# Product tiles of one step each, with a DMA transpose for every step, in an attention backward kernel

## The chip, the core and the metric

The kernel runs on one core of a Trainium2 chip. The metric is the device time of one execution in microseconds (us); lower is better. The time quoted for the kernel before is the median of three executions.

## What is computed

The reference runs a forward pass and its gradient. The forward pass takes a layer norm of `A_x` (2048 rows of 512), sends it through an attention block of 32 heads of 16 columns and through an MLP (512 to 1792 to 512, with gelu), gates one with the other and adds the input:

```python
def _A_ref(x, wqkv, wo):
    ...
    scores = jnp.einsum("bhqd,bhkd->bhqk", q, k) * (Dh ** -0.5)
    p = _softmax(scores, axis=-1)
    o = jnp.einsum("bhqk,bhkd->bhqd", p, v)
    ...
x = A_x
xn = _layernorm(x, axis=-1)
s = _A_ref(xn, A_wqkv, A_wo)
g = _silu(_B_ref(xn, B_w1, B_b1, B_w2, B_b2))
return x + s * g
...
_out, _vjp = jax.vjp(_f, A_x, A_wqkv, A_wo, B_w1, B_b1, B_w2, B_b2)
_grads = _vjp(grad_out)
```

The outputs are the forward result and seven gradients: of the input, the two attention weights, and the weights and biases of the MLP.

## The kernel before

The program has three stages. A first one (`Pre`) computes the norms, the projections, the MLP and the gradient that enters the attention. The middle one (`attention_core`) does the attention forward and backward in one sweep. The last one (`phase3`) forms the weight gradients and the gradient of the input. The schedule is written out by hand: each engine executes its instructions in the order in which the Python code emits them, and only semaphores hold an engine back.

The change lies in `attention_core`. Its work is cut into 64 blocks: 16 pairs of heads by 4 chunks of 512 queries. A block has 16 steps, one for each 128 keys (`kb` from 0 to 15), so there are 1024 steps, numbered `g`. A step handles 128 keys by 512 queries for both heads of a pair (`hj` 0 and 1):

- `emit_s`: TensorE forms the scores `s` (L906), and ScalarE takes their exponential into `et` (L912). One `et` tile holds four steps.
- `emit_d`: TensorE forms the gradient of the probabilities, `d` (L924).
- `emit_mult`: VectorE multiplies `d` with `et` into the product tile `gts` (L941), one instruction of 128x512 for each head. A `gts` tile holds two steps (an even and an odd `kb`), and the pool `gtp` has three such tiles.
- `emit_dmat`: after every odd `kb`, SyncE (SP) issues a DMA transpose (L956) of the whole `gts` tile, 128x2048 bf16, into a tile `gk` of the pool `gbp`. After every fourth step it also issues a DMA transpose `ekd` (L960) of one 128x512 part of `et`. So in four steps SP issues `gk`, `gk`, `ekd`.
- `emit_T` and `emit_cT`: TensorE transposes the other seven parts of `et` (L970), and ScalarE and VectorE copy them out as `ek` (L982).
- `emit_x`: TensorE accumulates `X` over the 16 steps (L1000, L1003, L1007); L1007 reads `gts`.
- `emit_xs`, `emit_XT`, `emit_fin`: once a block, `X` is copied out, transposed and finished by small GpSimd (POOL) operations at step 2 of the next block. These make the small weight tiles `W` (L1049 to L1055).
- `emit_z`: 20 steps behind, TensorE multiplies `gk` and `ek` by `W` into `Z` (L1080, L1088); `emit_acc` adds `Z` to an accumulator on VectorE (L1102).

A step's `gts` may be overwritten only when the DMA transpose that reads it has landed. L941 therefore waits for the landing of a transpose three tiles earlier, and the transpose on SP waits for the last of the products that it reads.

The operands of the next pair are loaded into a second set of tiles. The 13 loads are issued by POOL, one at a time, at steps 10, 14, 18, ... 58 counted from the first step of a pair. In front of each load POOL copies two elements of the current `gts` into `tick` (L1140), which holds the load back until VectorE has reached that step.

Other DMA transposes on SP are of use for comparison, because their sizes differ. `stg<-gp` (L679, in the last stage) is 128x2048 for the first three of its four column chunks, `CH = [(0, 4), (4, 4), (8, 4), (12, 2)]`, and 128x1024 for the fourth. `wT<-WKV_s` (L739) reads 128x1024 from device memory, and `wT<-in_A_wqkv_dram` (L738) 128x512.

Of the kernel before, what the change touches and what calls it, by code (L numbers as in the profile page):

```python
# [8 lines left out]
bf16 = mybir.dt.bfloat16  # L9
# [42 lines left out]
def op_load_list(k, t, p, ld):  # L52

    L = []
    for hj in range(2):
        h = 2 * p + hj
        L.append(lambda h=h, hj=hj: ld(out=t["KVT"][32 * hj + 1:32 * hj + 17, :], in_=k.KT_s[h * 16:h * 16 + 16, :]))
        L.append(lambda h=h, hj=hj: ld(out=t["QDT"][32 * hj + 1:32 * hj + 17, :], in_=k.QT_s[h * 16:h * 16 + 16, :]))
        L.append(lambda h=h, hj=hj: ld(out=t["QDT"][32 * hj:32 * hj + 1, :], in_=k.UT_s[h:h + 1, :]))
    for hj in range(2):  # L60
        h = 2 * p + hj
        L.append(lambda h=h, hj=hj: ld(out=t["KVT"][64 + 32 * hj:80 + 32 * hj, :], in_=k.VT_s[h * 16:h * 16 + 16, :]))
        L.append(lambda h=h, hj=hj: ld(out=t["QDT"][64 + 32 * hj:80 + 32 * hj, :], in_=k.DOT_s[h * 16:h * 16 + 16, :]))
    L.append(lambda: ld(out=t["NAT"][:].rearrange("q k j c -> q k (j c)"), in_=k.NAT_s[p]))
    L.append(lambda: ld(out=t["NATQq"][:].rearrange("q k j c -> q k (j c)"), in_=k.NATQq_s[p]))
    L.append(lambda: ld(out=t["NATQd"][:].rearrange("q k j c -> q k (j c)"), in_=k.NATQd_s[p]))
    return L
# [777 lines left out]
def attention_core(ctx, tc, k, Oall, dQall, dKVT_out, ident_f32, ident_bf, npairs=16, nqc=4):  # L845
    nc = tc.nc
    sb = lambda name, bufs: ctx.enter_context(tc.tile_pool(name=name, bufs=bufs, reuse_waits="tile"))
# [3 lines left out]
    ps_x = ctx.enter_context(tc.tile_pool(name="ps_x", bufs=1, space=PSUM, reuse_waits="tile"))  # L851
    ps_z = ctx.enter_context(tc.tile_pool(name="ps_z", bufs=1, space=PSUM, reuse_waits="tile"))
    etp = sb("etp", 3)
    gtp = sb("gtp", 3)
    gbp = sb("gbp", 12)
    ekd = sb("ekd", 6)
    ekc = sb("ekc", 7)
# [11 lines left out]
    tick = outp.tile([1, 2], bf16, name="tick")  # L869
# [12 lines left out]
    st_s, st_d, st_et, st_gt, st_T = {}, {}, {}, {}, {}  # L882
    blk = [dict(Gk={}, Ek={}) for _ in range(NB)]
    cur = {}

    def a_unit(g):
        return (g // 16, g % 16) if 0 <= g < NSTEP else None
# [6 lines left out]
    def op_of(j):  # L894
        return OP[blocks[j][0] % 2]

    def emit_s(g, hj):
        a = a_unit(g)
        if a is None:
            return  # L900
        j, kb = a
        op = op_of(j)
        qc = blocks[j][1]
        r = 32 * hj
        s = ps_st.tile([128, 512], f32, name="s", tag="st")
        nc.tensor.matmul(s[:], lhsT=op["KVT"][r:r + 32, kb * 128:(kb + 1) * 128], rhs=op["QDT"][r:r + 32, qc * 512:(qc + 1) * 512],  # L906
                         start=True, stop=True, tile_position=(r, 0))
        if hj == 0 and kb % 4 == 0:
            cur["et"] = etp.tile([128, 4, 2, 4, 128], bf16, name="et")
        et = cur["et"]  # L910
        st_et[g] = et
        nc.scalar.activation(out=et[:, :, hj, kb % 4, :], in_=s[:].rearrange("k (b q) -> k b q", b=4), func=ACT.Exp)  # L912

    def emit_d(g, hj):
        a = a_unit(g)
        if a is None:
            return
        j, kb = a
        op = op_of(j)
        qc = blocks[j][1]  # L920
        r = 64 + 32 * hj
        d = ps_d.tile([128, 512], f32, name="d", tag="d")
        st_d[g, hj] = d
        nc.tensor.matmul(d[:], lhsT=op["KVT"][r:r + 32, kb * 128:(kb + 1) * 128], rhs=op["QDT"][r:r + 32, qc * 512:(qc + 1) * 512],  # L924
                         start=True, stop=True, tile_position=(r, 0))
# [4 lines left out]
    def emit_mult(g):  # L930
        a = a_unit(g)
        if a is None:
            emit_cT(g - 1, 7 - VCOPY[(g - 1) % 16], 7, nc.vector.tensor_copy)
            return
        kb = a[1]
        if kb % 2 == 0:
            cur["gts"] = gtp.tile([128, 2, 2, 512], bf16, name="gts")
        gts = cur["gts"]
        st_gt[g] = gts
        for hj in range(2):  # L940
            nc.vector.tensor_tensor(out=gts[:, kb % 2, hj, :].rearrange("k (b q) -> k b q", b=4),  # L941
                                    in0=st_d.pop((g, hj))[:].rearrange("k (b q) -> k b q", b=4),
                                    in1=st_et[g][:, :, hj, kb % 4, :], op=ALU.mult)
            if hj == 0:
                emit_cT(g - 1, 7 - VCOPY[(g - 1) % 16], 7, nc.vector.tensor_copy)

    def emit_dmat(g):
        a = a_unit(g)
        if a is None:
            return  # L950
        j, kb = a
        kc = kb // 4
        if kb % 2 == 1:
            gk = gbp.tile([128, 2, 2, 4, 128], bf16, name="gk")
            blk[j]["Gk"][kb // 2] = gk
            nc.sync.dma_start_transpose(out=gk[:].rearrange("q r h b k -> q (r h b) k"), in_=st_gt[g][:].rearrange("k a h q -> k (a h q)"))  # L956
        if kb % 4 == 3:
            ek = ekd.tile([128, 4, 128], bf16, name="ekd")
            blk[j]["Ek"][(kc, 3)] = ek
            nc.sync.dma_start_transpose(out=ek[:], in_=st_et[g][:, 3, 1].rearrange("k a q -> k (a q)"))  # L960
# [15 lines left out]
    def emit_cT(g, lo, hi, copy):  # L976

        a = a_unit(g)
        if a is None or lo == hi:
            return  # L980
        j, kb = a
        copy(out=blk[j]["Ek"][kb // 4][:, kb % 4, lo:hi].rearrange("q i k -> q (i k)").bitcast(f32),  # L982
             in_=st_T[g][:, lo:hi].rearrange("q i k -> q (i k)").bitcast(f32))

    def emit_x(g, part):
        a = a_unit(g)
        if a is None:
            return
        j, kb = a
        if part == "e" and kb == 0:  # L990
            blk[j]["X"] = ps_x.tile([128, 512], f32, name="X", tag="X")
        X = blk[j]["X"]
        NATt = op_of(j)["NAT"]
        et = st_et[g]
        for c in range(4):
            half, hj = c // 2, c % 2
            r = 32 * c
            ev = et[:, half::2, hj, kb % 4, :]
            if part == "e":
                nc.tensor.matmul(X[r:r + 32, 0:256], lhsT=NATt[:, kb, hj, 1:33], rhs=ev,  # L1000
                                 start=(kb == 0), stop=False, skip_group_check=True, tile_position=(0, r))
            elif part == "l":
                nc.tensor.matmul(X[r:r + 32, 256:512], lhsT=Lc[:], rhs=ev,  # L1003
                                 start=False, stop=False, skip_group_check=True, tile_position=(0, r))
            else:
                gv = st_gt[g][:, kb % 2, hj, :].rearrange("k (b q) -> k b q", b=4)[:, half::2, :]
                nc.tensor.matmul(X[r:r + 17, 256:512], lhsT=NATt[:, kb, hj, 0:17], rhs=gv,  # L1007
                                 start=False, stop=(kb == 15), skip_group_check=True, tile_position=(0, r))

# [9 lines left out]
    def emit_XT(g):  # L1019
        j = g // 16 - 1  # L1020
        if g % 16 != FIN_AT or not 0 <= j < NB:
            return
        xs = blk[j].pop("xs")
        XT = ps_d.tile([128, 4, 128], f32, name="XT", tag="d")
        for qb in range(4):
            nc.tensor.transpose(XT[:, qb, :], xs[:, qb * 128:(qb + 1) * 128], ident_f32[:])
        blk[j]["XT"] = XT
# [84 lines left out]
    late = []  # L1112
    for hj in range(2):
        emit_s(0, hj)
    for g in range(NSTEP + 16 + 8):
        cur["g"] = g
        a = a_unit(g)
        if a is not None:
            j, kb = a
            p, qc = blocks[j]  # L1120
            if kb == 0 and qc == 0 and p + 1 < npairs:
                for i, f in enumerate(op_load_list(k, OP[(p + 1) % 2], p + 1, nc.gpsimd.dma_start)):
                    late.append((g + 10 + 4 * i, f))
        emit_s(g + 1, 0)
        emit_d(g, 0)
        emit_d(g, 1)
        emit_s(g + 1, 1)
        emit_T(g - 1)
        emit_XT(g)
        emit_z(g + ZOFF)  # L1130
        emit_x(g - 1, "e")
        emit_x(g - 1, "l")
        emit_x(g - 1, "g")
        emit_mult(g)
        emit_xs(g - 1)
        emit_fin(g)
        for it in [x for x in late if x[0] <= g]:
            late.remove(it)

            nc.gpsimd.tensor_copy(out=tick[:], in_=st_gt[g][0:1, kb % 2, 1, 510:512])  # L1140
            it[1]()
        emit_acc(g + ZOFF)
        emit_cT(g - 1, 0, 7 - VCOPY[(g - 1) % 16], nc.scalar.copy)
        st_T.pop(g - 1, None)
        emit_dmat(g)
        st_gt.pop(g - 2, None)
        st_et.pop(g - 12, None)
# [112 lines left out]
```

## Time and profile before

| | |
|---|---|
| median of three runs | 2374.84 us (2371.86 to 2382.14) |
| the profiled execution: time, span | 2376.85 us, 2375.1 us |
| first stage, `attention_core`, last stage (by the first and last rows of its tiles) | about 0 to 247, 247 to 1960, 1960 to 2375 us |
| TensorE (matmul) busy, whole span | 2186.0 us |
| VectorE busy, ScalarE busy | 1951.4 us, 1784.9 us |
| GpSimd busy | 619.5 us |
| granted TensorE clock, mean | 0.974 |
| data moved by DMA | 459.38 MB, mean 193 GB/s |

The profile shows one execution. A row of a group names the line, the engine, the operation and the tiles (`gts<-d,et` is written from `d` and `et`), then the number of instructions, their busy time and the mean of one, and the idle time in front of them with what ended it. SPq rows are the instructions of SP's queue: the duration of a DMA transpose there is the time that SP spends in issuing it, after its waits; the transfer itself ends later, and its landing is listed by tile. DMA queue q1 carries what SP issues, q0 what POOL issues, and the queues called "instruction" fetch program code. A "cycle" below is four steps.

### The profile page before, as it was taken

The page shows a single profiled execution, that of the slowest core. Times are in us where ns is not written, and L with a number is a line of the kernel's source. Part 1 is how long each engine was busy: PE and PEld are TensorE (multiplying, and loading weights), DVE is VectorE, ACT ScalarE, POOL GpSimd, SP SyncE. Part 2 cuts the span into 40 slices and gives each one's busy share as a digit, 9 for nine tenths or more (in the row PEclk, how much of TensorE's full clock was granted, in tenths as well). Part 3 has the DMA queues.
Part 4 walks back from the last instruction along what each step waited for, and adds up shares of the span by engine and source line. Part 5 has one row for each costly group of instructions (what it writes and reads, how often), then busy time and mean ns, then how long its engine had stood idle before and what let it go on. Part 6 is the DMA issues. An engine that isn't in the chain of part 4 may idle for free.

```text
span 2375.1 us, 79122 instructions
## 1 busy us (share of the span) xinstructions
PE 2186.0 (92%) x32738; PEld 1231.7 (52%) x32738; DVE 1951.4 (82%) x3760; ACT 1784.9 (75%) x3481; POOL 619.5 (26%) x1386
## 2 busy tenths in 40 slices
PE   6799899999999999999999999999999996698798
PEld 3444455555555555555555555555555553243353
DVE  5567799999999999999999999988999996687123
ACT  4554788988889888888988889888889976553112
POOL 4547322222222222221222223122222114200023
PEclk9999899999999999999999999999999998899899
DMA  6766899999999999999999999999999998694951
GB/s 216 228 223 213 177 193 185 199 194 188 192 195 192 187 193 191 196 188 191 192 188 193 194 197 191 189 185 187 195 198 198 191 184 274 159 264 134 261 171 52
DMA packets 1419418, 459.38 MB, mean 193 GB/s; under 512 B 1337134, under 2 KB 1401774, under 8 KB 1419056
## 3 DMA queue, kind: packets, MB, share of 16 engines
q1 hardware_dynamic: 1405008, 424.68, 93.9%
q0 software_dynamic: 12464, 28.06, 4.6%
q8 instruction: 256, 4.19, 0.7%
q10 hardware_dynamic: 1584, 1.57, 0.2%
q14 instruction: 106, 0.87, 0.1%
HBM read 60.69 MB, written 64.75 MB: 53 GB/s over the span
## 4 chain that ended last, share of the span: by engine, by line
PE 52%; DMA 18%; DVE 13%; ACT 8%; issue 4%; POOL 2%; SPq 2%; DVEq 0%; POOLq 0%; ACTq 0%
DMA gk<-gts 14%; PE tT L970 14%; PE s L906 8%; DVE gts L941 6%; PE Z L1080 5%; PE Z L1088 4%; ACT ek L982 3%; ACT et L912 3%; PE X L1000 3%; PE X L1003 3%; PE X L1007 3%; PE ps_dw L782 2%; PE ps_h L336 2%; PE ps_m L351 2%; PE ps_dw L606 1%
## 5 line engine op out<-in xcount | busy, mean ns | idle before, releaser
L941 DVE TENSOR_TENSOR gts<-d,et 128x512 bf16<-128x512 f32 x2048 | 1358.3, 683 | 129.6 <-DMA gk<-gts 48.4
L912 ACT ACTIVATE et<-s 128x512 bf16<-128x512 f32 x2048 | 1113.0, 595 | 140.1 <-PE s L906 89.7
L970 PE MATMUL tT<-ident_bf,et 128*128 128x128 bf16 x7168 | 574.2, 220 | 34.5 <-ACT ek L982 21.6
L970 PEld LDWEIGHTS <-et 128*128 128x128 bf16 x7168 | 440.9, 98 | 281.1 <-issue 272.6
L982 ACT COPY ek<-tT 128x320 f32<-128x320 f32 (+2 forms) x1024 | 479.8, 469 | 57.9 <-DVE ek L982 52.1
L906 PE MATMUL s<-QDT,KVT 32*128 32x512 bf16 x2048 | 458.2, 385 | 2.4 <-ACT et L912 1.7
L924 PE MATMUL d<-QDT,KVT 32*128 32x512 bf16 x2048 | 430.2, 387 | 24.1 <-DVE gts L941 22.9
L1003 PE MATMUL X<-et,Lc 128*32 128x256 bf16 x4096 | 292.0, 274 | 1.9 <-POOL Lc L866 1.9
L1000 PE MATMUL X<-et,NAT 128*32 128x256 bf16 x4096 | 292.0, 275 | 0.2 <-DVE xs L1016 0.2
L1007 PE MATMUL X<-gts,NAT 128*17 128x256 bf16 x4096 | 291.9, 274 | 0.0
L906 PEld LDWEIGHTS <-KVT 32*128 32x128 bf16 x2048 | 114.0, 91 | 269.9 <-issue 264.6
L1080 PE MATMUL Z<-gk,W 128*32 128x256 bf16 x4096 | 206.1, 279 | 5.4 <-DVE acc L1102 4.4
L1140 POOL COPY tick<-gts 1x2 bf16<-1x2 bf16 x195 | 34.0, 174 | 670.6 <-DVE gts L941 670.5
L1088 PE MATMUL Z<-ek,W 128*32 128x512 bf16 x1792 | 203.5, 391 | 0.1
L982 DVE COPY ek<-tT 128x128 f32<-128x128 f32 (+1 forms) x704 | 189.4, 269 | 0.2
L1049 POOL TENSOR_TENSOR W<-NATQq,rL 128x128 bf16<-128x128 bf16 x64 | 25.4, 397 | 555.8 <-DVE rL L1048 369.2
L1003 PEld LDWEIGHTS <-Lc 128*32 128x32 bf16 x4096 | 110.5, 97 | 51.9 <-POOL Lc L866 2.2
L1000 PEld LDWEIGHTS <-NAT 128*32 128x32 bf16 x4096 | 115.4, 97 | 12.7 <-issue 1.0
L1007 PEld LDWEIGHTS <-NAT 128*17 128x17 bf16 x4096 | 105.2, 92 | 2.4
L924 PEld LDWEIGHTS <-KVT 32*128 32x128 bf16 x2048 | 97.2, 91 | 4.3 <-issue 4.2
L1080 PEld LDWEIGHTS <-W 128*32 128x32 bf16 x4096 | 64.8, 94 | 58.7 <-issue 5.0
L592 ACT CAST ob_w<-ps_dw 128x512 bf16<-128x512 f32 (+1 forms) x22 | 12.4, 563 | 93.2 <-PE ps_dw L782 57.6
(193 smaller groups left out, 2461.5 us busy)
## 6 DMA issues: line engine op xcount, KB each, us to landing
gk<-gts SPq DMA_TRANSPOSE x512, 5.4
H1T_s<-h1r SPq DMA_DIRECT2D x28, 256.0 KB, 3.9
HGT_s<-hgT SPq DMA_DIRECT2D x8, 896.0 KB, 4.4
gp<-H1T_s SPq DMA_DIRECT2D x12, 512.0 KB, 5.0
DH_s<-stg SPq DMA_DIRECT2D x12, 512.0 KB, 3.5
hch<-DH_s SPq DMA_DIRECT2D x12, 512.0 KB, 7.8
out_dram<-ob_w POOLq DMA_DIRECT2D x42, 128.0 KB, 3.2
NAT_s<-NS SPq DMA_DIRECT2D x4, 1056.0 KB, 6.3
```

Of the source, the lines that this page charges most:

```text
L336: nc.tensor.matmul(ps[:], lhsT=w1_sb[:, ic, fc * 128:(fc + 1) * 128], rhs=yT[:, ic, g * 512:(g + 1) * 512], start=(ic == 0), stop=(ic == I ...
L906: nc.tensor.matmul(s[:], lhsT=op["KVT"][r:r + 32, kb * 128:(kb + 1) * 128], rhs=op["QDT"][r:r + 32, qc * 512:(qc + 1) * 512], start=True, ...
L912: nc.scalar.activation(out=et[:, :, hj, kb % 4, :], in_=s[:].rearrange("k (b q) -> k b q", b=4), func=ACT.Exp)
L924: nc.tensor.matmul(d[:], lhsT=op["KVT"][r:r + 32, kb * 128:(kb + 1) * 128], rhs=op["QDT"][r:r + 32, qc * 512:(qc + 1) * 512], start=True, ...
L941: nc.vector.tensor_tensor(out=gts[:, kb % 2, hj, :].rearrange("k (b q) -> k b q", b=4), in0=st_d.pop((g, hj))[:].rearrange("k (b q) -> k b ...
L970: nc.tensor.transpose(t[:, i, :], et[:, i // 2, i % 2, kk, :], ident_bf[:])
L982: copy(out=blk[j]["Ek"][kb // 4][:, kb % 4, lo:hi].rearrange("q i k -> q (i k)").bitcast(f32), in_=st_T[g][:, lo:hi].rearrange("q i k -> q ...
L1000: nc.tensor.matmul(X[r:r + 32, 0:256], lhsT=NATt[:, kb, hj, 1:33], rhs=ev, start=(kb == 0), stop=False, skip_group_check=True, tile_positi ...
L1003: nc.tensor.matmul(X[r:r + 32, 256:512], lhsT=Lc[:], rhs=ev, start=False, stop=False, skip_group_check=True, tile_position=(0, r))
L1007: nc.tensor.matmul(X[r:r + 17, 256:512], lhsT=NATt[:, kb, hj, 0:17], rhs=gv, start=False, stop=(kb == 15), skip_group_check=True, tile_pos ...
L1080: nc.tensor.matmul(Z[r:r + 32, h * 256:(h + 1) * 256], lhsT=WT[j % 2][1][:, qb, hj, :], rhs=blk[j]["Gk"][2 * kc + h][:, :, hj, qb, :], sta ...
L1088: nc.tensor.matmul(Z[r:r + 32, :], lhsT=WT[j % 2][0][:, qb, hj, :], rhs=mv, start=False, stop=(qb == 3), skip_group_check=True, tile_posit ...
```

## The change

The product tile now holds one step, and the pool has six of them instead of three tiles of two steps; the bytes are the same. After each step SP issues a DMA transpose of that step's 128x1024 into its half of `gk`. `gk` itself, its pool and its readers keep their shape, except that L1007 reads the new `gts`. The 13 operand loads of a pair move from steps 10, 14, 18, ... 58 to steps 6, 9, 12 and 15 of each block (6, 9, 12, 15, 22, 25, ... 54 from the first step of the pair).

```diff
-    gtp = sb("gtp", 3)
+    gtp = sb("gtp", 6)
...
         kb = a[1]
-        if kb % 2 == 0:
-            cur["gts"] = gtp.tile([128, 2, 2, 512], bf16, name="gts")
-        gts = cur["gts"]
+        gts = gtp.tile([128, 2, 512], bf16, name="gts")
         st_gt[g] = gts
         for hj in range(2):
-            nc.vector.tensor_tensor(out=gts[:, kb % 2, hj, :].rearrange("k (b q) -> k b q", b=4),
+            nc.vector.tensor_tensor(out=gts[:, hj, :].rearrange("k (b q) -> k b q", b=4),
...
-        if kb % 2 == 1:
-            gk = gbp.tile([128, 2, 2, 4, 128], bf16, name="gk")
-            blk[j]["Gk"][kb // 2] = gk
-            nc.sync.dma_start_transpose(out=gk[:].rearrange("q r h b k -> q (r h b) k"), in_=st_gt[g][:].rearrange("k a h q -> k (a h q)"))
+        if kb % 2 == 0:
+            cur["gk"] = gbp.tile([128, 2, 2, 4, 128], bf16, name="gk")
+            blk[j]["Gk"][kb // 2] = cur["gk"]
+        nc.sync.dma_start_transpose(out=cur["gk"][:, kb % 2].rearrange("q h b k -> q (h b) k"),
+                                    in_=st_gt[g][:].rearrange("k h q -> k (h q)"))
...
-                gv = st_gt[g][:, kb % 2, hj, :].rearrange("k (b q) -> k b q", b=4)[:, half::2, :]
+                gv = st_gt[g][:, hj, :].rearrange("k (b q) -> k b q", b=4)[:, half::2, :]
...
-                    late.append((g + 10 + 4 * i, f))
+                    late.append((g + 16 * (i // 4) + 6 + 3 * (i % 4), f))
...
-            nc.gpsimd.tensor_copy(out=tick[:], in_=st_gt[g][0:1, kb % 2, 1, 510:512])
+            nc.gpsimd.tensor_copy(out=tick[:], in_=st_gt[g][0:1, 1, 510:512])
```

## The prediction

> **What bounds the kernel now.** I read first the page's busy times and its chain of work, then the middle stage by itself, then SP's queue, since the change doubles the transposes that SP issues. The page says:
>
> ```profile
> PE 2186.0 (92%) x32738; PEld 1231.7 (52%) x32738; DVE 1951.4 (82%) x3760; ACT 1784.9 (75%) x3481; POOL 619.5 (26%) x1386
> ...
> q1 hardware_dynamic: 1405008, 424.68, 93.9%
> ...
> q8 instruction: 256, 4.19, 0.7%
> ...
> DMA gk<-gts 14%; PE tT L970 14%; PE s L906 8%; DVE gts L941 6%; PE Z L1080 5%; PE Z L1088 4%; ACT ek L982 3%; ACT et L912 3%; PE X L1000 3%; PE X L1003 3%; PE X L1007 3%; PE ps_dw L782 2%; PE ps_h L336 2%; PE ps_m L351 2%; PE ps_dw L606 1%
> ```
>
> The largest member of the chain is no engine but the transfer `gk<-gts`, and SP's DMA queue q1 is busy for 93.9% of the span. The busy times by stretch show the middle stage:
>
> ```profile
> 247.00:1960.00 1713.00, 1645.54 (x29935) 976.14 (x29938) 1578.51 (x3071) 1507.98 (x3072) 398.14 (x1129) 0.99 1.12 191
> ```
>
> The columns after the length are PE, PEld, DVE, ACT and POOL. DVE is busy 1578.5 of 1713 us, so 134 us at most could be won there before it binds. In the waits DVE loses to the transposes only
>
> ```profile
> DVE gts L941 <- DMA gk<-gts: 48.4, 56, 2.2
> ```
>
> SP is on no busy list, so I looked at its queue in order of time, start and duration first (x2 merges two issues and the gap between them):
>
> ```profile
> 999.94 4.79 SPq L956 DMA_TRANSPOSE gk<-gts  x2
> 1004.83 1.21 SPq L960 DMA_TRANSPOSE ekd<-et  x1
> 1006.13 5.77 SPq L956 DMA_TRANSPOSE gk<-gts  x2
> 1011.99 1.22 SPq L960 DMA_TRANSPOSE ekd<-et  x1
> 1013.31 5.03 SPq L956 DMA_TRANSPOSE gk<-gts  x2
> 1018.45 1.80 SPq L960 DMA_TRANSPOSE ekd<-et  x1
> 1020.34 4.64 SPq L956 DMA_TRANSPOSE gk<-gts  x2
> ```
>
> Three cycles last 1020.34 - 999.94 = 20.40 us, and SP is inside them for 4.79 + 1.21 + 5.77 + 1.22 + 5.03 + 1.80 = 19.82 us. SP is nearly full already. How long one issue takes by size is told by the rows of single tiles and lines (durations are minimum/median/maximum in ns):
>
> ```profile
> L956 SPq DMA_TRANSPOSE gk<-gts x512: 1590/2190/5047, 251.0 to 1952.1; - x171
> ```
> ```profile
> L960 SPq DMA_TRANSPOSE ekd<-et x256: 1189/1219/2455, 258.8 to 1954.2; - x128
> ```
> ```profile
> L739 SPq DMA_TRANSPOSE wT<-WKV_s x4: 1307/1307/1309, 2204.3 to 2212.3; - x4
> ```
> ```profile
> L679 SPq DMA_TRANSPOSE stg<-gp x16: 1340/1627/2962, 2106.2 to 2189.1; - x16
> ```
>
> The undisturbed issue is some 1.20 us for 128x512, 1.31 (L739) to 1.34 (the shortest of `stg`, one of its 128x1024 ones) for 128x1024, and 1.59 to 1.61 for 128x2048. That is a straight line with a fixed part: 1.20 + (1.60 - 1.20)/3 = 1.33 for 128x1024. Four times the data cost a third more; two issues of half the size cost 2.67 where one cost 1.60. The rest of the 2.19 us median of `gk` is SP held up by the transfers behind it. That shows in the DMA view of 1006 to 1016 us, 40 slices of 0.25 us:
>
> ```profile
> GB/s 276 287 185 0 0 114 290 291 290 289 289 288 231 53 240 216 88 0 0 0 0 6 9 9 137 293 290 286 293 280 289 217 0 0 209 291 292 287 291 293
> ...
> q8 instruction: 1, 0.02, 0.7%
> ```
>
> At full rate, some 290 GB/s, the 512 KB of one `gk` take 1.8 us. For almost 2 us (from 1010) nothing moves, in a stretch that holds one fetch of program code (q8); SP's second issue of that pair, at 1008.23, took 3.67 us, and `gts` L941 stood still in front of 1012.41. By the packet records the stage has 279 such stalls of half a microsecond or more, about one a cycle.
>
> **The change part by part.**
>
> *SP's issues.* A cycle takes away two `gk` issues and adds four halves. Gaps between issues are 0.09 to 0.10 us (1004.83 + 1.21 to 1006.13). The least that SP needs in a cycle is before 2 x 1.60 + 1.22 + 3 x 0.10 = 4.7 us, under the 6.65 us that a cycle takes (1704.4 us from the first issue at 251.0 to the end of the last at 1955.4, by 256 cycles), so stalls of up to 1.9 us have room. After it is 4 x 1.34 + 1.22 + 5 x 0.10 = 7.08 us. That alone exceeds the present cycle by 0.43 us; by 256 cycles, +109 us. Nothing hides it: SP has no other place in the program for these issues, and every one is needed to free a product tile. With 1.307 us and gaps of 0.09 the least is 6.87, +57 us: the lower end.
>
> *What of the stalls stays on SP.* Before, SP's excess over the undisturbed issue is 0.71 us for a mean `gk` (the 512 records' mean is 2.31) and 0.05 for a mean `ekd` (1.27 against 1.22), though `ekd` is issued right behind a `gk` whose data are still moving. SP is thus held when much is outstanding, and little when little is. A half has 256 KB, 0.9 us of transfer in an issue of 1.44 us with its gap, so the engines drain each before the next is pushed; a stall must first be longer than that slack. Ends: 5 x 0.05 = 0.25 us a cycle by the row of `ekd`, 2 x 0.71 = 1.42 by the row of `gk`, if each stall stays whole on SP. Below nothing is excluded, since the undisturbed issue is the least there is. I take 0.25, because with idle time between transfers a half resembles `ekd` more than two `gk` back to back: 256 x 0.25 = +64 us. The upper end is 364 us.
>
> *Product tiles.* DVE's instructions keep their number and shape (2048 by 683 ns). A tile comes free when its own half has landed, where it had to wait for the pair. This could give back the 48.4 us, but only while SP keeps up. When SP is last, DVE runs into the six tiles and waits for landings; behind L941 on DVE stand the copies `ek` (L982) and the accumulation (L1102), and through them PE and ACT wait. So I credit nothing. The six-step depth stays: six steps of 7.08/4 = 1.77 us are 10.6 us, and a landing now takes 5.4 us (median), so the loop does not bind by itself. In the built program each SP transpose also waits for the transpose eight issues before it; eight were 10.7 steps and are 6.4, still 11 us. Covered; only landings beyond 11 us would cost.
>
> *Loads.* Number and size are the same: 195 ticks of 174 ns and 195 issues of about 0.5 us on POOL, which is busy 398 of 1713 us in the stage. Every fourth load used to sit at step 2 of a block behind the finishing operations, and now none does; PE has waited for POOL's `W` for 2.0 us in all. The last load moves from step 58 to 54, so nothing is late. I cost it at nothing; if that cover failed, it would be 0.7 us in front of `W` 64 times, 45 us.
>
> The sum: 2376.85 + 109 + 64 = 2550 for the profiled execution; its time is 2 us above the median of the runs, so 2548.
>
> The Trainium skill, page "DMA: Bandwidth & Descriptors", section "Issuing engines are not separate DMA queues", calls the sequencer time of an issue "usually small relative to the DMA itself". By that rule SP would have room and the change would cost nothing. The trace differs: 1.6 us of issue stand against 1.8 us of transfer. The same page, section "Rules for kernel authors", says to coalesce many small transfers into one; it speaks against this change, without a price for SP.
>
> **The rivals.** (1) SP is not the limit, and the earlier release of tiles counts. This decides if a half issues in (6.65 - 1.22 - 0.50)/4 = 1.23 us or less. Then DVE's 48.4 us go and the time is 2328. For it speaks the 14% of `gk<-gts` in the chain; against it the three sizes, none of which allows 1.23 at 128x1024. 9%. (2) An issue shrinks with its bytes, because what is measured is mostly waiting: 2.19/2 = 1.1 us, a cycle needs 6.1 us, DVE still paces, and nothing changes: 2375. Against it: `ekd` at a quarter of the bytes takes 1.22. 3%. (3) Each stall holds SP as long as now: 109 + 364 = 473 us, 2848. For it: the fetches come with PE's instructions, whose number is unchanged. Against it: the row of `ekd`. 8%.
>
> **How the numbers follow.** The forecast, SP as the pace, has 80%. Its own range runs from 2376.85 + 57 = 2434, a little less for gains that I do not credit, to an excess of 0.835 us a cycle, the middle between the ends: 2376.85 + 109 + 214 = 2700. I say 2425 to 2700, which leaves the rivals out. About 0.5%, 12 us, is what a measurement of this kernel can tell from no change. Faster by more: 0.09. Within: 0.03. Slower: 0.88.
>
> **What the profile after would show.** Right: SP's queue without gaps over 0.1 us, 1024 `gk` issues with a minimum near 1.34 us and a median little above it, the middle stage longer by 110 to 330 us, DVE's wait for `gk<-gts` grown to a hundred us or more, DMA with idle slices between transfers. Wrong: gaps on SP in front of each half (rival 1 or 2), or a median issue of 1.7 us and more (rival 3). If the first or the last stage changes, I have missed something.

## The result, and the profile after

The changed kernel takes 2632.22 us (median of four runs, 2626.03 to 2632.38), the kernel before 2375.36 (median of the three runs above and a fourth): a ratio of 1.1071, 95% interval 1.1042 to 1.1101. The profiled execution took 2626.03 us with a span of 2624.3 us. The forecast was 2548 in a range of 2425 to 2700: the direction and the mechanism held, the size fell short by 84 us.

The page of the changed kernel, the same lines as before. TensorE's busy share falls, and so does that of the DMA queue, while the transfer `gk<-gts` takes a quarter of the chain in place of 14%:

```profile
PE 2286.1 (87%) x32689; PEld 1269.6 (48%) x32738; DVE 1958.3 (75%) x3760; ACT 1788.9 (68%) x3481; POOL 624.8 (24%) x1386
...
q1 hardware_dynamic: 1421392, 424.75, 85.1%
...
q8 instruction: 256, 4.19, 0.7%
...
DMA gk<-gts 25%; PE tT L969 10%; PE s L906 6%; DVE gts L939 5%; ACT ek L981 4%; PE Z L1087 3%; PE Z L1079 3%; ACT et L912 3%; PE X L999 2%; PE X L1002 2%; PE X L1006 2%; PE ps_dw L782 2%; DVE ek L981 2%; PE ps_h L336 1%; PE ps_m L351 1%
```

No engine and no DMA queue is fuller than before, so what paces the kernel is not on these lines. The busy times of the middle stage (from the first `gk` issue to the end of the last `ekd` issue; columns as in the prediction) say where the time is. Of the two lines, the first is the kernel before, the second the kernel after, each from its own answer:

```profile
251.00:1955.40 1704.40, 1639.65 (x29835) 972.85 (x29835) 1574.83 (x3066) 1504.40 (x3065) 390.22 (x1115) 0.99 1.12 192
```
```profile
251.00:2197.10 1946.10, 1740.08 (x29889) 1010.08 (x29889) 1583.75 (x3067) 1508.35 (x3065) 400.42 (x1128) 0.97 1.00 168
```

The stage is 241.7 us longer, while VectorE and ScalarE do the same work in the same busy time, within 0.6%. TensorE's busy time grows by 100 us with the same instructions, at a mean granted clock of 0.97 in place of 0.99; whether that is a cause or a consequence is asked below (F). The rest of the program starts the stage at the same 251.0 us and needs 427.2 us behind it in place of 419.7. A cycle of four steps went from 6.66 to 7.60 us. SP's queue in order of time (x4 merges four issues and the gaps between them):

```profile
1005.32 6.83 SPq L954 DMA_TRANSPOSE gk<-gts  x4
1012.24 1.23 SPq L959 DMA_TRANSPOSE ekd<-et  x1
1013.59 6.66 SPq L954 DMA_TRANSPOSE gk<-gts  x4
1020.36 1.20 SPq L959 DMA_TRANSPOSE ekd<-et  x1
1021.66 5.70 SPq L954 DMA_TRANSPOSE gk<-gts  x4
1027.45 1.22 SPq L959 DMA_TRANSPOSE ekd<-et  x1
```

From 1005.32 to 1028.77, where the next issue starts, SP pauses once, for 0.40 us at 1016.96; all other gaps are 0.09 to 0.12 us. Over the whole stage the median gap is 0.09 us, and only 22 gaps of 1279 exceed 0.15 us; before there were 213 of 767. The rows by tile:

```profile
L954 SPq DMA_TRANSPOSE gk<-gts x1024: 1231/1262/3092, 251.0 to 2194.6; - x171
```
```profile
L959 SPq DMA_TRANSPOSE ekd<-et x256: 1188/1219/2977, 258.4 to 2195.9; - x128
```

A half issues in 1.26 us at the median where a pair took 2.19, but there are twice as many. VectorE's wait for the landing has grown from 48.4 to 187.7 us, though each tile is now released by itself:

```profile
DVE gts L939 <- DMA gk<-gts: 187.7, 177, 3.4
```

And the DMA engines are idle more often. This is the view of 1006 to 1016 us, 40 slices:

```profile
GB/s 0 0 0 4 8 10 12 12 193 290 292 241 22 0 131 184 278 254 293 253 259 282 284 138 91 280 292 287 138 12 234 315 29 0 0 182 271 69 16 79
```

Counted from the packet records between 260 and 1950 us in slices of 0.1 us, fewer than four packets are under way on average in 15% of the slices, against 8% before, though the bytes are the same. Not all of it is waiting for SP: the first gap of the view, 1006 to 1008, is a stall like that in the view of before, in a stretch that holds one fetch. But no engine of the kernel is nearer to its limit than before, and SP has no room left.

### The profile page after: what moved, and what is told of

Same layout as the page of the kernel before. It is cut to its first block, busy times and chain, and to the rows that moved or that the text cites. A ratio compares the mean times of both kernels' runs of the same rounds, so it can differ in the third digit from the quotient of the medians.

```text
span 2624.3 us, 80432 instructions
## 1 busy us (share of the span) xinstructions
PE 2286.1 (87%) x32689; PEld 1269.6 (48%) x32738; DVE 1958.3 (75%) x3760; ACT 1788.9 (68%) x3481; POOL 624.8 (24%) x1386
## 3 DMA queue, kind: packets, MB, share of 16 engines
q1 hardware_dynamic: 1421392, 424.75, 85.1%
## 4 chain that ended last, share of the span: by engine, by line
PE 42%; DMA 28%; DVE 12%; ACT 8%; issue 5%; POOL 2%; SPq 1%; DVEq 0%; POOLq 0%; ACTq 0%
DMA gk<-gts 25%; PE tT L969 10%; PE s L906 6%; DVE gts L939 5%; ACT ek L981 4%; PE Z L1087 3%; PE Z L1079 3%; ACT et L912 3%; PE X L999 2%; PE X L1002 2%; PE X L1006 2%; PE ps_dw L782 2%; DVE ek L981 2%; PE ps_h L336 1%; PE ps_m L351 1%
## 5 line engine op out<-in xcount | busy, mean ns | idle before, releaser
L939 DVE TENSOR_TENSOR gts<-d,et 128x512 bf16<-128x512 f32 x2048 | 1357.7, 684 | 352.7 <-DMA gk<-gts 187.7
L969 PE MATMUL tT<-ident_bf,et 128*128 128x128 bf16 x7168 | 589.6, 224 | 62.7 <-ACT ek L981 52.6
L969 PEld LDWEIGHTS <-et 128*128 128x128 bf16 x7168 | 451.8, 99 | 310.7 <-issue 303.4
L924 PE MATMUL d<-QDT,KVT 32*128 32x512 bf16 x2048 | 493.9, 392 | 122.9 <-DVE gts L939 120.1
L906 PE MATMUL s<-QDT,KVT 32*128 32x512 bf16 x2048 | 517.8, 393 | 2.3 <-ACT et L912 1.6
L906 PEld LDWEIGHTS <-KVT 32*128 32x128 bf16 x2048 | 127.8, 91 | 414.5 <-issue 409.5
L1002 PE MATMUL X<-et,Lc 128*32 128x256 bf16 x4096 | 297.4, 279 | 1.8 <-POOL Lc L866 1.8
L999 PE MATMUL X<-et,NAT 128*32 128x256 bf16 x4096 | 297.6, 280 | 0.2 <-DVE xs L1015 0.2
L1087 PE MATMUL Z<-ek,W 128*32 128x512 bf16 x1792 | 209.7, 402 | 0.1
L1079 PEld LDWEIGHTS <-W 128*32 128x32 bf16 x4096 | 68.8, 94 | 72.6 <-issue 17.8
L924 PEld LDWEIGHTS <-KVT 32*128 32x128 bf16 x2048 | 98.0, 91 | 11.5 <-issue 11.4
L1087 PEld LDWEIGHTS <-W 128*32 128x32 bf16 x2048 | 53.2, 93 | 59.5 <-issue 15.7
```

What stands on the lines that cost most here:

```text
L939: nc.vector.tensor_tensor(out=gts[:, hj, :].rearrange("k (b q) -> k b q", b=4), in0=st_d.pop((g, hj))[:].rearrange("k (b q) -> k b q", b=4 ...
L969: nc.tensor.transpose(t[:, i, :], et[:, i // 2, i % 2, kk, :], ident_bf[:])
L1002: nc.tensor.matmul(X[r:r + 32, 256:512], lhsT=Lc[:], rhs=ev, start=False, stop=False, skip_group_check=True, tile_position=(0, r))
L1079: nc.tensor.matmul(Z[r:r + 32, h * 256:(h + 1) * 256], lhsT=WT[j % 2][1][:, qb, hj, :], rhs=blk[j]["Gk"][2 * kc + h][:, :, hj, qb, :], sta ...
L1087: nc.tensor.matmul(Z[r:r + 32, :], lhsT=WT[j % 2][0][:, qb, hj, :], rhs=mv, start=False, stop=(qb == 3), skip_group_check=True, tile_posit ...
```

## The experiments

The theory (A): SP issues the transposes one after the other, an issue has a price that hardly falls with its size, and the changed kernel asks for five a cycle in place of three, which is more than fits. The rivals: the new load steps (C), the single tiles and their waits (D), the DMA engines moving small transposes less well (B), TensorE (F).

**Which part of the change it is.** `loads_only` is the kernel before with

```diff
-                    late.append((g + 10 + 4 * i, f))
+                    late.append((g + 16 * (i // 4) + 6 + 3 * (i % 4), f))
```

> The kernel before with the new load steps alone. Theory A (SP's issues pace the middle stage, the loads cost nothing): 2363 to 2387 us, the same as before within 0.5%. Rival C (part of the 257 us comes from the loads, which now collide with other work): 2400 us or more.

Measured: 2369.83 us against 2384.67 of the kernel before on the same chip, ratio 0.9935 (0.9916 to 0.9954). The loads cost nothing; they are worth 15 us, a little more than the 0.5% expected at most. Where those come from the profile cannot say: it caught the slowest of the six executions, 2376.89 us, with a stage of 1702.2 us, 2 us less than before, and a wait of VectorE for `gk<-gts` of 46.3 us in place of 48.4.

`split_old_loads` is the changed kernel with that line put back.

> The changed kernel with the old load steps, that is the split alone. Theory A: SP paces either way, so the load steps do nothing: 2615 to 2655, within 1% of the changed kernel's ratio of 1.107. Rival C (the load steps are worth 15 us in either direction there too): 2600 or 2650 and beyond.

Measured: 2638.74 us, ratio 1.1086 (1.1046 to 1.1127); 1.1071 with the new load steps. The two intervals overlap, and the load steps cannot be told from nothing there. The split alone makes the whole loss.

`split_pair_tiles` keeps the three tiles of two steps and splits only the DMA:

```diff
-            nc.sync.dma_start_transpose(out=gk[:].rearrange("q r h b k -> q (r h b) k"), in_=st_gt[g][:].rearrange("k a h q -> k (a h q)"))
+            for r in range(2):
+                nc.sync.dma_start_transpose(out=gk[:, r].rearrange("q h b k -> q (h b) k"), in_=st_gt[g][:, r].rearrange("k h q -> k (h q)"))
```

> The kernel before with its three tiles of two steps and the old load steps, but each tile is transposed by two DMAs of 128x1024, both issued after the odd step. Theory A (what counts is the number of issues on SP, 5 a cycle): 2600 to 2700 us, as the changed kernel, since SP has to do the same. Rival D (the six single tiles are what costs: their waits and releases): back to 2375 to 2420 us.

Measured: 2632.54 us, ratio 1.1036 (1.1007 to 1.1065). The halves issue as in the changed kernel:

```profile
L957 SPq DMA_TRANSPOSE gk<-gts x1024: 1231/1263/3237, 251.7 to 2213.5; - x171
```

Tiles, waits and releases are those of the kernel before, and the loss is that of the changed kernel. D falls. It also shows that the release by single steps returned no time that can be seen: with it 1.1086 or 1.1071, without it 1.1036. VectorE's wait for the landings does differ, 237.4 us here against 180.1 in `split_old_loads`; with SP as the pace, that is no gain.

**Issues or data.** `no_ekd` takes one issue in five out of the changed kernel:

```diff
-        if kb % 4 == 3:
-            ek = ekd.tile([128, 4, 128], bf16, name="ekd")
-            blk[j]["Ek"][(kc, 3)] = ek
-            nc.sync.dma_start_transpose(out=ek[:], in_=st_et[g][:, 3, 1].rearrange("k a q -> k (a q)"))
...
-                        if qb == 3 and hj == 1:
-                            mv = blk[j]["Ek"][(kc, 3)][:]
-                        else:
-                            mv = blk[j]["Ek"][kc][:, :, 2 * qb + hj, :]
+                        mv = blk[j]["Ek"][kc][:, :, min(2 * qb + hj, 6), :]
```

> The changed kernel without the ekd transposes; the last part of et goes into Z from another part of ek (output not the reference's). 4 issues a cycle. Theory A: 7.60 us a cycle less 1.22 + 0.10 for the issue and some 0.2 of its stalls is 6.1 us, under the 6.65 of before, so SP no longer paces and the time falls to 2340 to 2420 us. Rival B (data): 11% of the data in the stage, 1946 x 0.11 = 214 us at the most: 2410 to 2500.

Measured: 2312.81 us, ratio 0.9694 (0.9676 to 0.9711), a little below the 2340 expected. The kernel still makes four issues a cycle, one more than the kernel before, and has lost only the 11% of the transposed data that `ekd` had; yet it is some 320 us faster than the changed kernel, where rival B allowed 214 at the most. The loss is more than undone. The cycle is 6.41 us, of which the four issues take 5.90 and their gaps 0.51: SP is still full, but no longer late. VectorE's wait all but ends:

```profile
DVE gts L939 <- DMA gk<-gts: 3.9, 9, 0.8
```

`plain_copy` leaves bytes, tiles, waits and the number of DMAs as in the changed kernel and replaces the kind:

```diff
-        nc.sync.dma_start_transpose(out=cur["gk"][:, kb % 2].rearrange("q h b k -> q (h b) k"),
-                                    in_=st_gt[g][:].rearrange("k h q -> k (h q)"))
+        nc.sync.dma_start(out=cur["gk"][:, kb % 2].rearrange("q h b k -> q (h b k)"),
+                          in_=st_gt[g][:].rearrange("k h q -> k (h q)"))
```

> The changed kernel with a plain DMA copy of the same 256 KB in place of each half transpose (output not the reference's); ekd stays a transpose. Bytes, number of issues, tiles and waits are the same; a plain issue took 0.32 to 0.57 us on SP elsewhere in the trace. Theory A: SP needs 4 x 0.45 + 1.22 + 0.5 = 3.5 us a cycle and is idle half the time; VectorE paces, 2300 to 2380 us. Rival B (it is the number of DMAs or their landings, whatever the kind): 2500 us or more.

Measured: 2311.94 us, ratio 0.9688 (0.967 to 0.9706). A plain issue of the same 256 KB holds SP 0.465 us at the median instead of 1.262:

```profile
L954 SPq DMA_DIRECT2D gk<-gts x1024: 464/465/2042, 249.3 to 1880.1; - x171
```

SP then idles 2.9 us of a cycle in gaps, and the stage is 1632.6 us long with VectorE busy 1576.6 of them. That is about what the stage takes when SP does not pace it:

```profile
249.30:1881.90 1632.60, 1604.52 (x29825) 959.54 (x29826) 1576.61 (x3063) 1499.42 (x3065) 393.79 (x1115) 1.00 0.67 200
```

So it is not the number of DMAs, of landings or of bytes that costs; it is that they are transposes. Whether their issue or their transfer is what costs, this run alone does not tell, since a plain copy also makes fewer packets (q1 is busy for 61.6% of the span in place of 85.1%). The next run does.

`tiny_extra` goes the other way and adds issues with almost no data to the kernel before:

```diff
+    tnp = sb("tnp", 4)
...
+            tiny = tnp.tile([128, 1, 128], bf16, name="tiny")
+            nc.sync.dma_start_transpose(out=tiny[:], in_=st_gt[g][:, 1, 1, 384:512])
```

> The kernel before, and behind each 128x2048 transpose one more of 128x128 into a tile that nobody reads: 5 issues a cycle, as in the changed kernel, but 6% more data (256 packets on 4608 a cycle). Theory A: the least on SP is 2 x 1.60 + 2 x 1.15 + 1.22 + 0.5 = 7.2 us a cycle, so the stage grows by 150 to 330 us: 2520 to 2700. Rival B (the DMA engines pace; small transposes only move less well): 6% of the transfers at the most, under 100 us: 2375 to 2475.

Measured: 2840.76 us, ratio 1.1911 (1.1886 to 1.1937), above the 2520 to 2700 expected. The direction is that of the theory, and B is out: with 6% more data the stage is 464 us longer where B allowed 100, and q1 is busy for only 76.7% of the span. The size was underestimated, in the issue and in what SP is held beyond it. The smallest transpose of these runs, 128x128, is not cheaper than one of 128x512:

```profile
L957 SPq DMA_TRANSPOSE gk<-gts x512: 1594/1682/5211, 250.6 to 2414.7; - x171
L959 SPq DMA_TRANSPOSE tiny<-gts x512: 1179/1232/3141, 252.3 to 2416.4; - x171
```

2 x 1.61 + 2 x 1.23 + 1.22 + 0.42 of gaps are 7.32 us a cycle; the cycle is 8.47. So 1.15 us a cycle are holds, where the expectation had room for 0.75 at the most. A hold is the time by which an issue lasts longer than an undisturbed one of its size.

**The price by size.** `unequal_split` is `split_pair_tiles` with the pair cut into 2 and 14, 4 and 12, 6 and 10, 8 and 8 blocks of 128x128 in turn:

```diff
+            m = 2 * (kb // 2 % 4 + 1)
+            for lo, hi in ((0, m), (m, 16)):
...
```

> As split_pair_tiles, but the pair is cut unequally: 2 and 14, 4 and 12, 6 and 10, 8 and 8 blocks of 128x128 in turn. It reads the issue by size. If the price is a straight line through 1.20 at 4 blocks and 1.60 at 16 (as in the prediction), the undisturbed issues are 1.13, 1.20, 1.27, 1.33, 1.40, 1.47, 1.53 us for 2, 4, ... 14 blocks. If up to 8 blocks or so there is only the fixed part and a small slope (1.26 at 8 in the changed kernel), and beyond that SP waits for room, the slope is flat up to 8 to 10 and steeper above. Time as split_pair_tiles within 1.5%.

Measured: 2680.59 us, ratio 1.1232 (1.1212 to 1.1252), 1.8% over `split_pair_tiles` and so just outside what I expected. Medians of SP's issue from the single records of the trace, 128 of each size (256 for 8 blocks, 256 `ekd` of 4 blocks elsewhere), in us:

| blocks of 128x128 | 2 | 4 | 6 | 8 | 10 | 12 | 14 | 16 (`gk` before, shortest tenth) |
|---|---|---|---|---|---|---|---|---|
| issue | 1.20 | 1.25 | 1.25 | 1.26 | 1.36 | 1.44 | 1.51 | 1.62 |

This is no straight line. Up to 8 blocks the price is all but fixed, 1.2 to 1.26 us, and from there it rises by some 0.04 us a block. Two halves cost 2.52 where one whole costs 1.61, and cuts of 2 and 14 cost 2.71. What happens at 8 blocks the runs do not tell.

**The holds.** In the changed kernel the issues take 5.65 + 1.44 us a cycle by the means of the trace's records, against 4 x 1.262 + 1.219 = 6.27 undisturbed: 0.82 us of holds, 211 us in the stage. If the fetches of TensorE's program code make them, fewer TensorE instructions must make fewer. `fewer_pe`:

```diff
+            if part != "g" and kb > 0:
+                continue
             if part == "e":
                 nc.tensor.matmul(X[r:r + 32, 0:256], lhsT=NATt[:, kb, hj, 1:33], rhs=ev,
```

> The changed kernel with the matmuls of L999 and L1002 only in the first step of a block (output not the reference's): 7.5 of some 29 matmuls a step are left out, and with them a quarter of TensorE's program code. The excess of SP's issues in the changed kernel is some 0.83 us a cycle over 4 x 1.26 + 1.22. Theory A with stalls made by the fetches of TensorE's code: 64 fetches fewer of about 250, a quarter of 0.83 x 256 = 212 us: 2632 - 53 = 2580, and not lower than 2550, since SP still paces. Rival E (the stalls come from the transposes themselves, as many as there are DMAs): no change, 2620 to 2640. Rival F (TensorE paces): 8 x 0.11 us a step gone, 2400 us or less.

Measured: 2585.02 us, ratio 1.0836 (1.0802 to 1.087); expected 2580. The code fetches fell as meant, and the stage is 41 us shorter:

```profile
q8 instruction: 196, 3.21, 0.6%
...
249.40:2154.60 1905.20, 1655.81 (x22209) 852.20 (x22209) 1573.35 (x3067) 1499.22 (x3065) 398.67 (x1128) 0.93 0.97 171
```

The holds fell to (5.604 + 1.328) - 6.27 = 0.66 us a cycle, 170 us in the stage, by 20%; the fetches within the stage fell from 234 to 174, by 26%. The records of the two traces show where the holds lie. In the changed kernel 28% of SP's issues are under way within 1.5 us after the start of a fetch, and these carry 195 of the 211 us of holds; windows of the same length 3.5 us later carry 8. In `fewer_pe` 21% of the issues carry 148 of the 170 us. So a fetch costs SP 195/234 = 0.83 us in the one and 148/174 = 0.85 in the other; counted alike it is 1.04 in `tiny_extra`. Rival E falls. F falls too: a quarter of TensorE's matmuls is gone, and only the 41 us of the holds came back. Around the start of a fetch some 20 packets of q1, which otherwise take 18 ns at the median, last longer than 0.7 us. Why a fetch does this, no run shows.

**The other direction and the gain that was there.** `two_quad_tiles` has two tiles of four steps and one transpose of 128x4096 for each:

```diff
-    gtp = sb("gtp", 3)
-    gbp = sb("gbp", 12)
+    gtp = sb("gtp", 2)
+    gbp = sb("gbp", 5)
...
-        if kb % 2 == 1:
+        if kb % 4 == 3:
...
```

> The opposite direction: two product tiles of four steps, one transpose of 128x4096 each, 2 issues a cycle (gk tiles of four steps, five of them). SP needs one issue of some 2.3 to 2.5 us, 1.22 and 0.2, under 4 us a cycle, so its queue has room; but a tile of four steps comes free only when 1 MB has landed, some 3.7 us of data and 3 to 4 us around it, against four steps (6.4 us) of other work. If the release binds: 2420 to 2600. If the number of issues is all that counts: 2320 to 2380.

Measured: 2472.96 us, ratio 1.0404 (1.0369 to 1.0438), in the range named for the case that the release binds. SP waits 1.44 us a cycle in gaps, so its queue has room here, and VectorE loses 135.2 us to the landings, the longest 4.6:

```profile
DVE gts L941 <- DMA gk<-gts: 135.2, 93, 4.6
```

The size of an issue was misjudged once more: 4.15 us at the median, not 2.3 to 2.5.

```profile
L956 SPq DMA_TRANSPOSE gk<-gts x256: 3906/4152/5953, 257.0 to 2047.8; - x128
```

That the release binds is not quite shown: the five `gk` tiles hold 20 steps where twelve held 24, and no run separates the two.

`four_pair_tiles` gives the kernel before a fourth tile of two steps and no issue more:

```diff
-    gtp = sb("gtp", 3)
-    gbp = sb("gbp", 12)
+    gtp = sb("gtp", 4)
+    gbp = sb("gbp", 11)
```

> The kernel before with four tiles of two steps in place of three (and 11 gk tiles in place of 12, for room). If the release of product tiles was worth anything in the kernel before, it is had here without more issues: VectorE's wait of 48.4 us for gk<-gts goes, and 2320 to 2360 us result. If SP's queue holds it all the same: 2365 to 2385.

Measured: 2349.88 us against 2385.48, ratio 0.9865 (0.982 to 0.991). With `four_pair_loads` below it is the fastest of the kernels here that compute all that the reference does. The profile is of the fastest of its four executions, 2335.73 us; there VectorE's wait falls from 48.4 to 17.2 us, and the stage to 1664.0:

```profile
DVE gts L941 <- DMA gk<-gts: 17.2, 23, 1.6
```

Its cycle of 6.50 us is full of SP's issues: 4.87 for `gk`, 1.28 for `ekd`, 0.35 of gaps. So SP with the transfers behind it is next there too. That what is left up to the 1632.6 us of `plain_copy` lies in it is likely, but not shown. `four_pair_loads` adds the new load steps to it.

> The kernel before with four tiles of two steps (11 gk tiles) and the new load steps, the two edits that were each a little faster alone (0.9865 and 0.9935). If they add: 0.980, about 2337 us where the kernel before takes 2385. If the gain of the load steps was taken from the same waits: 0.986, as four_pair_tiles alone. Theory A sets a floor: SP's 2 x 1.61 + 1.22 + 0.3 = 4.7 us and about 1.4 us of holds a cycle are 6.1, VectorE needs about 6.38 (plain_copy), so not under 2300.

Measured: 2350.94 us against 2378.03, ratio 0.9878 (0.9853 to 0.9902), the same as without them. Whatever the load steps gained alone does not add.

## Why the prediction was right, and where it fell short

*SP as the pace* was right. Most of its marks came: a stage longer by 242 us where 110 to 330 were named, 1024 issues with a median hardly above the minimum, DVE's wait grown past a hundred, more idle slices of the DMA engines. Two came only nearly: the minimum of an issue is 1.231 us and not near 1.34, and 375 of the 1279 gaps exceed 0.1 us, though only 42 exceed 0.11. `split_pair_tiles`, `no_ekd` and `tiny_extra` change the number of issues each in its own way, and the time moves as this needs.

*The half's issue* was mis-sized: 1.34 us by the shortest `stg` of that size, with a straight line through 128x512 and 128x2048 that gave 1.33; measured 1.262, since the price is nearly flat up to 8 blocks. The undisturbed cycle is 4 x 1.262 + 1.22 + 0.51 = 6.78, not 7.08, and this term +31 us, not +109. The row of `wT<-WKV_s` at 1.307, read as the lower end, was the better neighbour, and still too high. The lower end has a slip besides: with 1.307 and gaps of 0.09 the sum is 6.90 and not 6.87, +63 us and not +57.

*The holds* are the term that was furthest off: 0.25 us a cycle by the row of `ekd`, +64 us; measured 0.82, +211 us. The bounds 0.25 and 1.42 held, the choice between them did not. The reason given, that a small issue is held little, is refuted by `ekd` itself: unchanged in size, its mean went from 1.27 to 1.44 us, a hold of 0.22, and a half's is 0.15. A hold is mostly the price of a fetch and falls on whichever issue is under way. Before, 25 of the 234 fetches of the stage start during an `ekd` issue, after the change 48. That its place behind a long `gk`, which took the hold first, is what spared it before is argued, not shown.

Together 31 + 211 = 242 us, the growth of the stage. This sum closes by itself, since issues, holds and gaps are all that a cycle of SP is made of; that fewer or cheaper issues and fewer fetches shorten it is what the runs show. The two errors were opposite in sign, and that the forecast missed by no more than 84 us is in part luck: with the half's issue right and the holds at 0.25, it would have named a growth of 95 us in place of 173. Another 7.5 us lie behind the stage, which the prediction did not have; the other kernels here need between 417 and 428 us there, so this may be no effect of the change. And the median stands 6 us above the profiled run.

*Product tiles* and *loads* were costed at nothing, rightly: `split_pair_tiles` and `split_old_loads`. The 48.4 us of rival 1 were real, as `four_pair_tiles` shows, but they are not to be had with more issues: a half issues in 1.26, over the 1.23 from which that rival decided. Rival 2 fell with the table by size. Rival 3, every hold whole at 1.42, is out as well: the measured 0.82 lies midway between 0.25 and 1.42, just under the 0.835 to which the range reached.

On the rule of the Trainium skill that the prediction weighed (page "DMA: Bandwidth & Descriptors", section "Issuing engines are not separate DMA queues"): it fits the plain copies here, 0.465 us of issue where 2.9 us pass from issue to landing at the median. It does not fit the transposes: 1.26 us of issue for 256 KB that, by an estimate from the 290 GB/s of the trace, move in 0.9 us, and that land 3.7 us after their issue.

## What to carry to other kernels

The issuing queue is a resource like an engine, though no busy line shows it: add up its issues and gaps for one period of the loop before splitting a DMA in it. A DMA transpose had a price per issue here that hardly shrank with its size below 128x1024, so what a split wins in release times must be set against that price; here another buffer won some of it without a further issue. A disturbance of a queue costs time where the queue has no room for it: the holds' 211 us were part of the loss here, and the undisturbed issue does not show them.

## What was unexpected of the hardware

A DMA transpose from one place of the on-chip memory to another took SP 1.17 us at the least in these runs and 1.23 at the median even for 128x128; the price is nearly flat up to 128x1024 (1.26) and then rises, to 1.6 for 128x2048 and 4.15 for 128x4096. A plain DMA of 128x1024 took it 0.465. Each fetch of 16 KB of program code by queue q8 cost SP 0.83 to 0.85 us in the changed kernel and `fewer_pe`, and 1.04 in `tiny_extra`. So TensorE's instruction count slowed a queue that TensorE never touches: with a quarter fewer of its matmuls the stage of the changed kernel was 41 us shorter, without TensorE being the pace.
